# Layer 2 in the written order on five engines, with its other work placed between products

## The chip, the cores and the metric

One core of a Trainium2 chip runs the whole program in one launch. The metric is the device time of one execution in microseconds (us). The core has five instruction queues that matter here: PE (matmuls), ACT (activations, copies), DVE (tensor arithmetic), POOL (tensor arithmetic too, and some DMAs in the attention), SP (here it issues nearly all DMAs). Each queue runs its instructions strictly in its own order; an instruction that waits for another engine's result, or for a buffer, holds up everything behind it on its queue.

## The reference

Attention on q, k, v gives 2304 tokens of 512 values; two feed-forward layers follow, each 512 to 2048 to 512, the second with ELU.

```
def _moe_ref(x, w_in, w_out):
    h = x @ w_in
    g = h * (1.0 / (1.0 + np.exp(-1.702 * h)))
    return (g @ w_out).astype(np.float32)

def _moe2_ref(x, w_in, w_out):
    h = x @ w_in
    g = np.where(h > 0.0, h, np.exp(np.minimum(h, 0.0)) - 1.0)
    return (g @ w_out).astype(np.float32)

def reference(**kwargs):
    attn_out = _attn_ref(**attn_kwargs)
    B, H, S, D = attn_out.shape
    x = np.ascontiguousarray(attn_out.transpose(0, 2, 1, 3)).reshape(B * S, H * D)
    x = _moe_ref(x=x, **moe_kwargs)
    return _moe2_ref(x=x, **moe2_kwargs)
```

## The kernel before

The program runs attention, layer 1 (which overlaps it) and layer 2. Every large matmul operand is split in two parts, hi (ACT copies it to fp32r, a rounded type that TensorE takes) and lo (DVE subtracts hi from the original), and each product is three matmuls: hi by hi, hi by lo, lo by hi. So an operand is ready only after a load, an ACT instruction and a DVE instruction. This pair is called a split below.

Layer 2 is computed block by block, with 7 products in place of 8 for a 2 by 2 block matrix (`PRODUCTS`). The operands of the 7 products are the four blocks A12, A22, A11, A21 and four sums of them, S1 to S4; on the weights' side likewise the blocks and the sums T1 to T3 and N4.

- The tokens are cut in three super blocks, `sb` = 0, 1, 2, each two halves of 256, 384 and 512 tokens (`SUPER`). The hidden dimension is cut in 8 pairs, `p` = 0 to 7.
- First multiplication: one **group** (p, sb) is 7 products, k = 0 to 6, of 6 matmuls each (`group_h2`, line 912). A group's matmuls need `ws` of its p (`split_w7`, L899 on ACT and L900 on DVE; `sum_w7`, L857, forms its four sums) and `xops` of its sb (`load_x`, `sum_x` at L866, `split_x2` at L887/L888). ACT copies the products k = 0 and 4 out of the PSUM bank, DVE adds the other five (L950). Then ELU: Relu and Exp on ACT (L906, L907), the end on DVE (L910), for two of the four quarters ("most") and later for the other two ("rest"); POOL makes the four sums S of the result (L866), and H and S are stored to DRAM (L929, L930) in the memory `gd`. There are 3 H buffers and 2 S buffers: a group's ELU writes into the S buffer, so it waits until the store of two groups earlier has landed.
- Order of groups: (0,0), (1,0), (0,1), (1,1), (0,2), (1,2), then p = 2 to 6 with sb 0, 1, 2, and last (7,1), (7,0), (7,2).
- Second multiplication: for sb = 1, 0, 2 and k = 0 to 6 there are 4 parts (`product_o2`, L1001). A part needs `gs`, the split of a piece `gf` of `gd` (`load_g` L962, `split_g` L968/L969), and `wo(k)`, the split of a 1 MB weight `wof` (`load_wo` L976, `split_wo` L981/L982). The weights are loaded once, while sb = 1 runs; `wof` has one buffer, so the load for k + 1 waits for the DVE half of the split for k.

What sets the order: within layer 2, PE alone runs in the order of the program (`tc.manual_schedule(engines={PE})`, line 1149). On ACT, DVE, POOL and SP a scheduler that has its own idea of durations places the instructions. The last part of a group (rest of ELU, sums, stores) is a function `last`, called once after product 1 of the next group. The operand `xops` of sb 2 is written into the program after group (1,0): four units of 256 columns, one buffer, sums on DVE. At the end of layer 1, in its last block of tokens (steps (5, 0), (5, 1), ...), the scheduler mixes the units of sb 0 (4 of 128 columns, one buffer `xs`, sums on POOL) with layer 1's own ACT and DVE work: g (L704 on ACT, L707 on DVE), which a matmul `h` waits for since h has two PSUM buffers.

## Time and profile before

| quantity | us |
|---|---|
| median of 3 runs | 1065.36 (1062.88 to 1068.53) |
| profiled execution, its own time | 1068.55 |
| its span | 1066.7 |
| PE busy | 962.2 (90% of the span) |
| DVE, ACT, POOL busy | 639.5, 535.3, 243.6 |
| last matmul ends (from the span's start) | 1059.85 |
| layer 2's first matmul starts | 602.77 |

The page cuts the span in 40 slices of 26.7 us; the first rows are PE's busy tenths and the granted TensorE clock in tenths of 2.4 GHz.

```
PE   8988999999999999999999989872898999738999997
PEclk8998999999999999999999995989999869999999
```

PE is busy nearly everywhere, apart from the slices about 600 to 690 and 815 to 880 us, which are the start of layer 2 and the passage from its first to its second multiplication. The clock is low in the same slices. A stage table (busy time of each engine in a stretch) is the view that the reader needs most: the length of a stretch less PE's work there is what a better order could win.

### The profile page before, as it was taken

How to read it: one execution, taken by the hardware profiler on the slowest of the kernel's cores; microseconds unless marked ns; L12 is line 12 of the kernel's file. 1: busy time of each engine (PE TensorE's matmuls, PEld its weight loads, DVE VectorE, ACT ScalarE, POOL GpSimd, SP SyncE). 2: the span in 40 equal slices, each digit the busy share in tenths (PEclk: the TensorE clock that was granted, in tenths of full speed). 3: DMA queues.
4: the chain of work that ended last, by engine and by line, in shares of the span. 5: the costliest groups of instructions: out<-in, count | busy, mean ns of one | idle time of the engine just before them, and what ended most of it. 6: DMA issues, size and time to landing. Idle time of an engine off the chain costs nothing.

```text
span 1066.7 us, 17803 instructions
## 1 busy us (share of the span) xinstructions
PE 962.2 (90%) x6820; PEld 827.0 (78%) x6820; DVE 639.5 (60%) x1029; ACT 535.3 (50%) x1110; POOL 243.6 (23%) x261
## 2 busy tenths in 40 slices
...
PEclk8998999999999999999999995989999869999999
...
GB/s 183 210 163 143 249 40 140 121 146 132 135 152 146 146 112 127 112 301 153 1 60 21 99 131 120 90 174 188 200 183 180 250 220 227 199 187 237 214 182 139
DMA packets 166325, 165.74 MB, mean 155 GB/s; under 512 B 83552, under 2 KB 131296, under 8 KB 165344
## 3 DMA queue, kind: packets, MB, share of 16 engines
...
## 4 chain that ended last, share of the span: by engine, by line
PE 59%; DVE 13%; DMA 10%; ACT 9%; issue 5%; POOL 3%; SPq 0%; POOLq 0%; DVEq 0%; ACTq 0%
PE h L694 15%; PE y L727 14%; PE o2d L1001 4%; PE o2a L1001 3%; PE o2c L1001 3%; PE h2c L937 3%; DMA wof<-wodram 3%; PE h2d L937 3%; PE h2a L937 3%; DMA gf<-gd 2%; DMA w64i<-in_moe_w_in_dram 2%; POOL S L866 2%; PE qk L456 2%; PE busy L778 2%; DMA xs<-ydram 2%
## 5 line engine op out<-in xcount | busy, mean ns | idle before, releaser
L727 PE MATMUL y<-g1h,whl1o 128*128 128x256 f32 (+1 forms) x768 | 216.7, 350 | 2.3 <-ACT g1h L708 1.7
L694 PE MATMUL h<-xh,whl1i 128*128 128x256 f32 (+1 forms) x768 | 172.7, 349 | 6.9 <-DVE g L707 5.3
L727 PEld LDWEIGHTS y<-g1h,whl1o 128*128 128x128 f32 x768 | 135.8, 192 | 21.9 <-issue 4.1
L694 PEld LDWEIGHTS h<-xh,whl1i 128*128 128x128 f32 x768 | 122.4, 191 | 26.1 <-DVE g L707 5.9
L383 POOL DMA_DIRECT2D vd<-in_v_dram x72 | 88.3, 1353 | 223.9 <-PE pv L559 84.5
L727 PE MATMUL y<-g1l,whl1o 128*128 128x256 f32 (+1 forms) x384 | 130.8, 341 | 0.8 <-DVE g1l L709 0.8
L969 DVE TENSOR_TENSOR gs<-gf,gs 128x768 fp32r<-128x768 f32 (+2 forms) x84 | 80.0, 963 | 72.8 <-ACT gs L968 72.5
L968 ACT ACTIVATE gs<-gf 128x768 fp32r<-128x768 f32 (+2 forms) x84 | 70.4, 844 | 86.9 <-DMA gf<-gd 28.3
L937 PE MATMUL h2a<-xops,ws 128*128 128x256 f32 (+2 forms) x288 | 64.5, 362 | 30.2 <-ACT xops L887 22.2
L694 PE MATMUL h<-xl,whl1i 128*128 128x256 f32 (+1 forms) x384 | 89.7, 345 | 0.0
L704 ACT ACTIVATE g<-h 128x512 f32<-128x512 f32 x72 | 43.0, 599 | 86.4 <-PE h L694 77.2
L707 DVE SCALAR_TENSOR_TENSOR g<-g,h 128x512 f32<-128x512 f32 x72 | 49.0, 682 | 62.1 <-ACT g L704 62.0
L937 PEld LDWEIGHTS h2a<-xops,ws 128*128 128x128 f32 x288 | 51.6, 206 | 36.5 <-ACT xops L887 23.1
L727 PEld LDWEIGHTS y<-g1l,whl1o 128*128 128x128 f32 x384 | 73.7, 192 | 7.3 <-DVE g1l L709 1.2
L866 POOL TENSOR_TENSOR S<-H 128x256 f32<-128x256 f32 (+2 forms) x48 | 49.6, 1057 | 130.1 <-DVE H L910 130.1
L937 PE MATMUL h2c<-xops,ws 128*128 128x256 f32 (+2 forms) x288 | 62.0, 353 | 17.4 <-DVE H L950 17.0
L1001 PE MATMUL o2a<-wo,gs 128*128 128x256 f32 x432 | 57.4, 296 | 17.8 <-DMA gf<-gd 13.9
L1001 PEld LDWEIGHTS o2a<-wo,gs 128*128 128x128 f32 x432 | 55.9, 204 | 19.1 <-ACT gs L968 14.9
L708 ACT ACTIVATE g1h<-g 128x512 fp32r<-128x512 f32 x72 | 45.6, 634 | 48.7 <-DVE g L707 47.9
L857 POOL TENSOR_TENSOR w7i<-w7i 128x256 f32<-128x256 f32 x32 | 26.0, 834 | 190.1 <-DMA w7i<-wdi 189.5
L937 PEld LDWEIGHTS h2c<-xops,ws 128*128 128x128 f32 x288 | 49.2, 199 | 24.9 <-DVE H L950 20.8
L694 PEld LDWEIGHTS h<-xl,whl1i 128*128 128x128 f32 x384 | 61.6, 192 | 6.5 <-issue 0.2
...
## 6 DMA issues: line engine op xcount, KB each, us to landing
...
```

The source lines that it names most:

```text
L383: nc.gpsimd.dma_start(out=self.vd[:, :, j, :], in_=src, accum_op=ALU.add)
L694: nc.tensor.matmul(out=ph[:, i, :], lhsT=w_in(1, f, c, wp), rhs=xp[:, c, :], start=(n == 0), stop=(n == 3 * NK - 1),)
L704: nc.scalar.activation(out=g, in_=ph, func=AF.Tanh, scale=0.851)
L707: nc.vector.scalar_tensor_tensor(out=g, in0=g, scalar=1.0, in1=ph, op0=ALU.add, op1=ALU.mult)
L708: nc.scalar.activation(out=gh, in_=g, func=AF.Copy)
L727: nc.tensor.matmul(out=yps[blk][m // nf][:, m % nf, :], lhsT=w_out(1, f, wp)[:, m, :], rhs=gp[:, i, :], start=(st == 0 and n == 0 and m % ...
L857: engine.tensor_tensor(out=at[out_], in0=at[a_], in1=at[b_], op=ALU.subtract)
L866: engine.tensor_tensor(out=s_[:, out_], in0=x, in1=y, op=op)
L937: nc.tensor.matmul(out=ps, lhsT=w[:, wp, slot, c * P:(c + 1) * P], rhs=x[:, xp, c, xi, :], start=(k < 4 and i == 0), stop=(i == 5), skip_g ...
L968: nc.scalar.activation(out=t[:, 0], in_=f, func=AF.Copy)
L969: nc.vector.tensor_tensor(out=t[:, 1], in0=f, in1=t[:, 0].bitcast(F32), op=ALU.subtract)
L1001: nc.tensor.matmul(out=ps[:, ch], lhsT=g[:, gp, j, ch * P:(ch + 1) * P], rhs=woops[k][:, wp, p], start=(k < 4 and p == 0 and i == 0 and ch ...
```

## The change

The change is one of order and of buffers; the sums and products are the same.

1. **Written order.** In layer 2's first multiplication all five engines run in the order of the program (`engines=EVERY`). A group's last part is cut in stages: `last(k)` is called after every product k of the next group: Relu and Exp of the rest at k = 1, its end on DVE and the sums on POOL at k = 2, the store of H at k = 4, that of S at k = 6. Other work is a list of tasks `background`, one after a product of a group: `add(i, k, task)` puts it behind product k of group i.
2. **xops of sb 2.** Eight units of 128 columns with 3 buffers in place of four of 256 with one; unit u is loaded at product 3u, counted from group (0,0), summed on POOL (before: DVE) at 3u + 3, split at 3u + 6.
3. **End of layer 1.** The units of sb 0 get two buffers, are summed on DVE (before: POOL) and are written into the steps (5, 1) to (5, 5) of the last block; `ws` of p = 0 and its sums move there too, from POOL to DVE. Of the units of sb 1, every other one is summed on POOL; three buffers.
4. **Weights of layer 2.** Their four sums go from POOL to DVE, their split stands after product 5 of a later group, the next load at product 6.
5. **Second multiplication.** The pieces `gf`/`gs` of sb 1 live in three buffers of `oeg` on the other side of the memory, which is free before the first multiplication ends; loads run four parts ahead, splits two; the first two weights and pieces are placed in groups (7,0) and (7,2).

```diff
...
     def elu(h, e, rows):
 
         nc.scalar.activation(out=e[:, rows], in_=h[:, rows], func=AF.Relu, scale=-1.0)
         nc.scalar.activation(out=e[:, rows], in_=e[:, rows], func=AF.Exp, scale=-1.0)
 
-        def rest():
-            nc.vector.scalar_tensor_tensor(
-                out=h[:, rows], in0=e[:, rows], scalar=-1.0, in1=h[:, rows], op0=ALU.add, op1=ALU.max
-            )
-
-        return rest
-
-    def group_h2(p, sb, pool):
+    def elu_end(h, e, rows):
+        nc.vector.scalar_tensor_tensor(
+            out=h[:, rows], in0=e[:, rows], scalar=-1.0, in1=h[:, rows], op0=ALU.add, op1=ALU.max
+        )
+
+    MOST, REST = slice(1, 3), slice(0, 4, 3)
+
+    def group_h2(p, sb, pool, before, background):
+
...
-        def last():
-            elu(h, s_, slice(0, 4, 3))()
-            sums(nc.gpsimd, s_, h, A12)
-            nc.sync.dma_start(out=gdram[sb][A12:, :, p, :].rearrange("o p n -> p o n"), in_=h[:, :3])
-            nc.sync.dma_start(out=gdram[sb][:A12, :, p, :].rearrange("o p n -> p o n"), in_=s_)
+        def last(k):
+            if k == 1:
+                elu(h, s_, REST)
+            elif k == 2:
+                elu_end(h, s_, REST)
+                sums(nc.gpsimd, s_, h, A12)
+            elif k == 4:
+                nc.sync.dma_start(out=gdram[sb][A12:, :, p, :].rearrange("o p n -> p o n"), in_=h[:, :3])
+            elif k == 6:
+                nc.sync.dma_start(out=gdram[sb][:A12, :, p, :].rearrange("o p n -> p o n"), in_=s_)
 
...
                 nc.scalar.activation(out=c21, in_=ps, func=AF.Copy)
             elif k == 4:
                 nc.scalar.activation(out=c11, in_=ps, func=AF.Copy)
-                most = elu(h, s_, slice(1, 3))
+                elu(h, s_, MOST)
             else:
...
-            if k == 1 and pending:
-                pending.pop(0)()
-            if k == 5:
-                most()
-        pending.append(last)
+            before(k)
+            if k == 6:
+                elu_end(h, s_, MOST)
+            for task in background.get(k, ()):
+                task()
+        return last
...
-            with tc.tile_pool(name="xs", bufs=1, side="right") as xs:
-                for c in range(2):
-                    for at in range(0, 256, P):
-                        load_x(0, c, at, P, xs)
-                        sum_x(nc.gpsimd, 0, c, at)
-                        split_x2(0, c, at)
-            sum_w7(nc.gpsimd, "i", w7[0])
-            split_w7(0, wa)
-            w7[1] = load_w7(wa, "i", 1)
-            sum_w7(nc.gpsimd, "i", w7[1])
+        elif wa is not None and blk == NBLK - 1:
+
+            if 1 <= f2 <= len(units):
+                load_x(*units[f2 - 1], P, xs0)
+            if 2 <= f2 <= len(units) + 1:
+                sum_x(nc.vector, *units[f2 - 2])
+                split_x2(*units[f2 - 2])
+            if f2 == len(units) + 1:
+                lxs.close()
+            if f2 == 1:
+                sum_w7(nc.vector, "i", w7[0])
+                split_w7(0, wa)
+            if f2 == 2:
+                w7[1] = load_w7(wa, "i", 1)
+            if f2 == 3:
+                sum_w7(nc.vector, "i", w7[1])
...
+            w7[2] = load_w7(wa, "i", 2)
+            with tc.tile_pool(name="xs1", bufs=3, side="right") as xs:
                 for at in range(0, 384, P):
                     for c in range(2):
                         load_x(1, c, at, P, xs)
-                        sum_x(nc.vector, 1, c, at)
+                        sum_x((nc.vector, nc.gpsimd)[c], 1, c, at)
                         split_x2(1, c, at)
-            w7[2] = load_w7(wa, "i", 2)
...
-    xs2 = l2.enter_context(tc.tile_pool(name="xs2", bufs=1, side="left"))
+    xs2 = l2.enter_context(tc.tile_pool(name="xs2", bufs=3, side="left"))
...
+    background = [{} for _ in groups]
+
+    def add(i, k, task):
+        i, k = i + k // 7, k % 7
+        background[i].setdefault(k, []).append(task)
+
+    units = [(2, c, at) for at in range(0, 512, P) for c in range(2)]
+    for u, unit in enumerate(units):
+        at = 3 * u
+        add(0, at, lambda unit=unit: load_x(*unit, P, xs2))
+        add(0, at + 3, lambda unit=unit: sum_x(nc.gpsimd, *unit))
+        add(0, at + 6, lambda unit=unit: split_x2(*unit))
+
+    def load_next(p):
+        w7[p] = load_w7(wa, "i", p)
+
+    add(0, 2, lambda: sum_w7(nc.vector, "i", w7[2]))
+    for p in range(NPAIR - 2):
+
+        i = groups.index((p, 2)) + 1 if p != 1 else groups.index((2, 1))
+        add(i, 5, lambda p=p: split_w7(p + 2, wa if p % 2 == 0 else wb))
+        if p + 3 < NPAIR:
+            add(i, 6, lambda p=p: load_next(p + 3))
+            add(i + 1, 6, lambda p=p: sum_w7(nc.vector, "i", w7[p + 3]))
+
+    with tc.manual_schedule(engines=EVERY):
+        before = lambda k: None
+            before = group_h2(p, sb, hpool2, before, background[i])
...
+                oeg = ltail.enter_context(tc.tile_pool(name="oeg", bufs=3, side="right"))
+                j = i + 1
+                add(j, 0, lambda: load_wo(0, wa))
                 for part in range(2):
-                    load_g(1, 0, part, oeg)
-                    split_g(1, 0, part, oeg)
-        for last in pending:
-            last()
+                    add(j, 2, lambda part=part: load_g(1, 0, part, oeg))
+                add(j, 6, lambda: split_wo(0, oe, "wo0"))
+                add(j, 6, lambda: load_wo(1, wa))
+                add(j + 1, 0, lambda: split_g(1, 0, 0, oeg))
+                add(j + 1, 2, lambda: split_g(1, 0, 1, oeg))
+                add(j + 1, 3, lambda: split_wo(1, wa, "ws"))
+                add(j + 1, 3, lambda: load_wo(2, wa))
+                add(j + 1, 4, lambda: load_g(1, 0, 2, oeg))
+                add(j + 1, 6, lambda: load_g(1, 0, 3, oeg))
+        split_g(1, 0, 2, oeg)
+        for k in range(7):
+            before(k)
...
+        order = [(sb, k) for sb in (1, 0, 2) for k in range(7)]
+        sequence = [(sb, k, part) for sb, k in order for part in range(4)]
+        loads, splits = sequence[4:], sequence[3:]
...
+        for i, (sb, k) in enumerate(order):
             for part, _ in enumerate(product_o2(sb, k, opool, op)):
 
                 at = sequence.index((sb, k, part))
+                while loads and sequence.index(loads[0]) <= at + 4:
+                    load_g(*loads[0], oeg if loads.pop(0)[0] == 1 else gp)
                 while splits and sequence.index(splits[0]) <= at + 2:
-                    split_g(*splits.pop(0), gp)
-                    if loads:
-                        load_g(*loads.pop(0), gp)
+                    split_g(*splits[0], oeg if splits.pop(0)[0] == 1 else gp)
...
```

The line numbers in the second kernel are higher: L704 to L737 and L866 to L888 are as before, the copies and additions L943, L945 and L950 become L952, L954 and L959, Relu and Exp L906/L907 become L909/L910, `gs` L968 becomes L978, `wo` L981 becomes L991, `wof` L976 becomes L986, `gf` L962 becomes L972.

On ACT at the end of layer 1, from the first unit of sb 0 (`xops_6150`, named by its `xs` unit) to the first g of block 5, before:

```order
L887 ACTIVATE xops_6150<-xs_0_0_6154 128x7x128
L736 ACTIVATE ye_4_6095<-y_4_5592 128x512
L736 ACTIVATE ye_4_6101<-y_4_5593 128x512
L736 ACTIVATE ye_4_6107<-y_4_5594 128x512
L887 ACTIVATE xops_6150<-xs_0_128_6163 128x7x128
L704 ACTIVATE g_5_0_6135<-h_5_0_6110 128x512
L704 ACTIVATE g_5_1_6233<-h_5_1_6208 128x512
```

and now:

```order
L887 ACTIVATE xops_6150<-xs_0_0_6189 128x7x128
L887 ACTIVATE xops_6150<-xs_1_0_6257 128x7x128
L736 ACTIVATE ye_4_6101<-y_4_5593 128x512
L736 ACTIVATE ye_4_6107<-y_4_5594 128x512
L704 ACTIVATE g_5_0_6135<-h_5_0_6110 128x512
L708 ACTIVATE g1h_0_6137<-g_5_0_6135 128x512
```

In both, two units stand ahead of the first g. Before, the second was xs_0_128, which shares one buffer with the first; now it is xs_1_0, which has a buffer of its own.

On POOL at the start of layer 2, where `xs` are the units and `S_0`, `S_1` the sums of a group of sb 0 or 1, before:

```order
L866 TENSOR_TENSOR xs_0_128_6163<-xs_0_128_6163 128x128 x4
L866 TENSOR_TENSOR xs_1_0_6172<-xs_1_0_6172 128x128 x4
L866 TENSOR_TENSOR xs_1_128_6181<-xs_1_128_6181 128x128 x4
L857 TENSOR_TENSOR w7i_6647<-w7i_6647 128x256 x4
L866 TENSOR_TENSOR S_0_6725<-H_0_6724 128x256 x2
L866 TENSOR_TENSOR S_0_6725<-S_0_6725,H_0_6724 128x256
L866 TENSOR_TENSOR S_0_6725<-H_0_6724,S_0_6725 128x256
L866 TENSOR_TENSOR S_0_6783<-H_0_6782 128x256 x2
L866 TENSOR_TENSOR S_0_6783<-S_0_6783,H_0_6782 128x256
L866 TENSOR_TENSOR S_0_6783<-H_0_6782,S_0_6783 128x256
```

and now:

```order
L866 TENSOR_TENSOR xs_0_0_6738<-xs_0_0_6738 128x128 x4
L866 TENSOR_TENSOR xs_1_0_6770<-xs_1_0_6770 128x128 x4
L866 TENSOR_TENSOR S_0_6726<-H_0_6725 128x256
L866 TENSOR_TENSOR S_0_6726<-S_0_6726,H_0_6725 128x256
L866 TENSOR_TENSOR S_0_6726<-H_0_6725 128x256
L866 TENSOR_TENSOR S_0_6726<-H_0_6725,S_0_6726 128x256
L866 TENSOR_TENSOR xs_0_128_6803<-xs_0_128_6803 128x128 x4
L866 TENSOR_TENSOR xs_1_128_6846<-xs_1_128_6846 128x128 x4
L866 TENSOR_TENSOR xs_0_256_6879<-xs_0_256_6879 128x128 x4
L866 TENSOR_TENSOR S_0_6807<-H_0_6806 128x256
L866 TENSOR_TENSOR S_0_6807<-S_0_6807,H_0_6806 128x256
L866 TENSOR_TENSOR S_0_6807<-H_0_6806 128x256
L866 TENSOR_TENSOR S_0_6807<-H_0_6806,S_0_6807 128x256
L866 TENSOR_TENSOR xs_1_256_6919<-xs_1_256_6919 128x128 x4
```

The four sums of group (0,0), then those of (1,0), now stand among the units of sb 2, of which eight are to be done; before, POOL did the units of sb 0 and nothing of sb 2.

On ACT in the second multiplication, sb 1, where `gs_k_part` is the split of a piece and `wo` that of a weight, before:

```order
L968 ACTIVATE gs_1_0_8520<-gf_1_0_8471 128x768
L981 ACTIVATE wo_8796<-wof_8700 128x2048
L968 ACTIVATE gs_1_1_8543<-gf_1_1_8477 128x768
L1011 ACTIVATE ot_1_8567<-o2a_8473 128x3x256
L968 ACTIVATE gs_1_2_8570<-gf_1_2_8500 128x768
L968 ACTIVATE gs_1_3_8593<-gf_1_3_8523 128x768
L981 ACTIVATE wo_8894<-wof_8799 128x2048
L968 ACTIVATE gs_2_0_8621<-gf_2_0_8546 128x768
L968 ACTIVATE gs_2_1_8644<-gf_2_1_8573 128x768
L968 ACTIVATE gs_2_2_8669<-gf_2_2_8596 128x768
L981 ACTIVATE wo_8992<-wof_8897 128x2048
```

and now, from the weight of k = 2 on:

```order
L991 ACTIVATE wo_8633<-wof_8454 128x2048
L978 ACTIVATE gs_2_0_8658<-gf_2_0_8605 128x768
L978 ACTIVATE gs_2_1_8681<-gf_2_1_8628 128x768
L978 ACTIVATE gs_2_2_8706<-gf_2_2_8656 128x768
L978 ACTIVATE gs_2_3_8729<-gf_2_3_8679 128x768
L991 ACTIVATE wo_8732<-wof_8636 128x2048
L978 ACTIVATE gs_3_0_8757<-gf_3_0_8704 128x768
L978 ACTIVATE gs_3_1_8780<-gf_3_1_8727 128x768
L978 ACTIVATE gs_3_2_8805<-gf_3_2_8755 128x768
L978 ACTIVATE gs_3_3_8828<-gf_3_3_8778 128x768
L991 ACTIVATE wo_8831<-wof_8735 128x2048
```

Before, the three weights of these rows (k = 4 to 6) follow each other after three or four pieces each, and all are ahead of the pieces of k = 2 and 3. Now one weight stands behind the four pieces of each k, so that the weight of k + 1 is split while product k runs.

On SP at the same place (`gf` are the loads of pieces, `wof` those of weights), before:

```order
L976 DMA wof_8700<-wodram 128x2048
L962 DMA gf_1_1_8477<-gd_101 128x768
L962 DMA gf_1_2_8500<-gd_101 128x768
L962 DMA gf_1_3_8523<-gd_101 128x768
L976 DMA wof_8799<-wodram 128x2048
L962 DMA gf_2_0_8546<-gd_101 128x768
L962 DMA gf_2_1_8573<-gd_101 128x768
L962 DMA gf_2_2_8596<-gd_101 128x768
L976 DMA wof_8897<-wodram 128x2048
L962 DMA gf_2_3_8624<-gd_101 128x768
```

and now:

```order
L972 DMA gf_2_0_8605<-gd_101 128x768
L972 DMA gf_2_1_8628<-gd_101 128x768
L986 DMA wof_8636<-wodram 128x2048
L972 DMA gf_2_2_8656<-gd_101 128x768
L972 DMA gf_2_3_8679<-gd_101 128x768
L972 DMA gf_3_0_8704<-gd_101 128x768
L972 DMA gf_3_1_8727<-gd_101 128x768
L986 DMA wof_8735<-wodram 128x2048
L972 DMA gf_3_2_8755<-gd_101 128x768
L972 DMA gf_3_3_8778<-gd_101 128x768
```

The last two pieces of each k now stand behind the weight of k + 1.

## Rows read from the trace of the kernel before

**Rows 1.** Stages: us, busy (count) of PE, PEld, DVE, ACT, POOL; PEclk, DMA share, GB/s.
```profile
602.80:715.40 112.60, 77.61 (x378) 68.34 (x379) 68.63 (x103) 48.89 (x62) 40.64 (x43) 0.82 0.38 131
...
715.40:815.80 100.40, 91.59 (x506) 82.43 (x505) 62.89 (x88) 56.19 (x77) 59.01 (x60) 0.98 0.53 189
...
815.80:848.00 32.20, 24.39 (x127) 21.21 (x125) 21.94 (x27) 17.76 (x24) 16.62 (x13) 0.93 0.65 226
...
848.00:887.80 39.80, 22.10 (x145) 21.23 (x145) 16.28 (x12) 15.60 (x14) 7.04 (x4) 0.71 0.63 228
...
887.80:936.40 48.60, 45.10 (x362) 44.49 (x363) 26.72 (x28) 19.71 (x23) 0.00 (x0) 0.96 0.63 198
...
936.40:980.40 44.00, 41.90 (x339) 40.42 (x337) 22.11 (x33) 18.51 (x29) 0.00 (x0) 1.00 0.60 204
```

**Rows 2.** Chain that ended last, in order of time: start, us, what.
```profile
722.33 0.71 PE h2d L937 x6
...
723.05 1.04 PE h2a L937 x6
...
731.72 1.40 PE h2b L937 x6
...
851.41 5.77 POOL S L866 x3
...
859.02 7.25 DMA wof<-wodram
...
879.70 4.75 DMA wof<-wodram
...
919.13 8.64 PE o2c L1001 x72
```

**Rows 3.** Timeline at layer 1's end: start, us, engine, line, op [idle before <-releaser].
```profile
552.20 0.92 SPq L876 DMA_DIRECT2D xs<-ydram  x2
...
555.38 1.82 POOL L866 TENSOR_TENSOR xs<-xs 128x128 f32<-128x128 f32 x4 [5.32 <-DMA xs<-ydram]
...
557.24 0.95 ACT L887 ACTIVATE xops<-xs 128x896 fp32r<-128x896 f32 x1 [2.92 <-POOL xs L866]
...
559.96 0.99 PE L694 MATMUL h<-xh,whl1i 128*128 128x256 f32 x4 [4.04 <-DVE g L707]
...
561.61 1.91 PE L694 MATMUL h<-xh,whl1i 128*128 128x256 f32 x8
```

**Rows 4.** Timeline of PE at the start of layer 2.
```profile
608.19 1.65 PE L937 MATMUL h2a<-xops,ws 128*128 128x256 f32 x6 [2.28 <-ACT H L943]
...
660.83 1.22 PE L937 MATMUL h2a<-xops,ws 128*128 128x512 f32 x2 [8.07 <-ACT xops L887]
```

**Rows 5.** Groups by line and form: busy us, mean ns | idle before.
```profile
L866 POOL TENSOR_TENSOR S<-H 128x256 f32<-128x256 f32 x16 | 11.5, 739 | 21.2 <-DVE H L910 21.2
...
L866 POOL TENSOR_TENSOR S<-H,S 128x256 f32<-128x256 f32 x8 | 7.9, 993 | 0.6
...
L866 POOL TENSOR_TENSOR xs<-xs 128x128 f32<-128x128 f32 x16 | 7.0, 459 | 54.0 <-DMA xs<-ydram 53.7
...
L887 ACT ACTIVATE xops<-xs 128x896 fp32r<-128x896 f32 x10 | 9.4, 949 | 17.0 <-POOL xs L866 10.5 <-DVE xs L866 6.4
...
L888 DVE TENSOR_TENSOR xops<-xs,xops 128x896 fp32r<-128x896 f32 x10 | 11.3, 1146 | 19.0 <-ACT xops L887 19.0
...
L982 DVE TENSOR_TENSOR wo<-wof,wo 128x2048 fp32r<-128x2048 f32 x7 | 16.9, 2408 | 27.1 <-ACT wo L981 27.1
```

**Rows 6.** Timeline of ACT in the second multiplication, sb 1.
```profile
866.28 1.91 ACT L981 ACTIVATE wo<-wof 128x2048 fp32r<-128x2048 f32 x1 [14.32 <-DMA wof<-wodram]
...
868.10 2.29 ACT L968 ACTIVATE gs<-gf 128x768 fp32r<-128x768 f32 x3
...
884.48 1.91 ACT L981 ACTIVATE wo<-wof 128x2048 fp32r<-128x2048 f32 x1 [4.24 <-DMA wof<-wodram]
...
886.88 2.73 ACT L968 ACTIVATE gs<-gf 128x768 fp32r<-128x768 f32 x3 [0.49 <-DMA gf<-gd]
```

42 lines of the change are left out of this document (11 added, 31 removed).

## The prediction

> **What bounds the kernel now.** I read the granted clock and the share of PE first: PE is busy nearly all the time, so only stretches where it stands still, or runs at half clock, can give anything. The stage table then says which [rows 1]. PE's pure work there is a count: at full clock a product of 6 matmuls takes 0.72, 1.04 or 1.40 us (256, 384, 512 columns) and one of 72 in the second multiplication of sb 1 takes 8.64 [rows 2], so a group takes 5.0, 7.3 or 9.8 and a whole p 22.1. From layer 2's first matmul to the start of (3,0) there are 9 groups, 66.4 us of products in 112.6: 46 us are lost. p = 3 to 6 take 100.4, or 25.1 each for 22.1. p = 7 takes 32.2 for 22.1. The second multiplication of sb 1 takes 39.8 + 48.6 = 88.4 for 7 products of 8.64, or 60.5. sb 0 takes 44.0 for about 40. sb 2 has no idle time and the change leaves it so.
>
> Then the timelines and the chain, for what each loss waits on. At layer 1's end PE stands 4.04 us, then runs 8 matmuls in 1.91 us, half rate [rows 3]. At layer 2's start PE stops for ACT's copy, and the 6 matmuls behind the stop span 1.65 us, twice the usual [rows 4]; the granted clock is 0.82 over this stage [rows 1]. Later it waits for xops of sb 2, which come through one buffer, the last time 8.07 us. At the passage to the second multiplication the chain goes through POOL's sums and weight loads [rows 2].
>
> **The change part by part.** Before's profiled execution is the base: 1068.55 us, 3.2 above the median, so differences are taken from it and applied to the median.
>
> *Layer 1's end.* SP's unit load of 552.20, late since the one buffer was full, gives POOL's sums at 555.38, ACT's split at 557.24, and behind that on ACT the first g, which h waits for until 559.96 [rows 3]. The order now has two units of separate buffers ahead of g, which can both be loaded long before, so g waits for no unit and PE need not stop or lose its clock. At most this saves 4.04 and the half rate: 4 matmuls in 0.99 and 8 in 1.91, at 0.12 each (8.64 by 72) 0.5 and 1.0 too long, 1.5 together. Later units still stand ahead of other g's and wait on loads, for which I take off 0.5: **-5.0**, bounds -5.5 and 0 (the wait comes back at the next g).
>
> *Start of layer 2.* POOL's sums become the path to xops of sb 2. Eight units are 32 x 0.459 = 14.7 us; in the written order the sums of (0,0) and (1,0) (about 4 x 0.74 = 3.0 each) and (0,1) (half as much again, 4.4) stand among them [rows 5]: 25.1 us. The first unit's load waits for memory that the last split of sb 1 frees, which I place some 11 us into layer 2, with 3 to 4 us to load it: POOL starts at about 617.5, an estimate, and would end at 642.6. But each of these S sums waits for a group's ELU end, and so for PE's own stops, while units behind it lie ready. I put 8 us on these waits, an estimate: three groups each have 2 to 4 us of stops, like the 2.28 at 608 [rows 4]. With 0.95 + 1.15 for the last split [rows 5] it makes 652.7, and with half a product's delay on the way some 654.5, where before (0,2) got its last wait over at 660.83 [rows 4] and a lo part 2 us later: -8.4. Of it 2.3 go again up to (3,0). The split of p = 2 has one `ws` buffer and can start only when (1,2) is done: seven eighths of a `wo` split, 1.7 on ACT and 2.1 on DVE [rows 5, 6], 4 us with PE idle. And the Relu of (2,1) waits for the store of (1,2), put at 3. With half rate behind both that is some 11 us of the 13.1 lost from (0,2) to (3,0); before lost 11 there (52.5 less 41.7 of products). Sum **-6.1**, bounds +2 (all of it lost in the waits) and -16 (no waits on POOL).
>
> *p = 3 to 6.* POOL is busy 59.0 of 100.4 us [rows 1]; the S buffers still are two, and the store of S still gates the Relu two groups later. Taking the weight sums off POOL brings the sums forward, but the stores now are issued after product 4 and 6. I find no net: **0**, bounds -10 (2.5 of the 3.0 us lost per p) and +4.
>
> *p = 7.* The weights and pieces are placed from (7,0) on. What was lost, 10.1, becomes about 6.9: stops on H and S stores in (7,2), and half clock: **-3.2**. *sb 1, k = 0 and 1.* PE now waits at part 2 of k = 0 (its piece is queued on SP behind `wof` of k = 2, which waits for DVE's split of k = 1), some 8 us, and at k = 1 (its piece behind the store of S(7,2), which waits for POOL's sums, 5.77 for three ops before [rows 2]), some 10; before lost 22.5 (39.8 less 17.3). **-1.2**. For both together bounds -9 and +6.
>
> *sb 1, k = 2 to 6.* Here the written order costs. Before, weights were split well ahead of their products (the order has those of k = 4 to 6 in front of most pieces of k = 2), so that k = 3 to 6 ran at 8.64 each [rows 2]. Now a loop closes: DVE ends `wo(k+1)`; only then SP issues `wof(k+2)`, 4.75 to landing when alone [rows 2]; two pieces are queued behind it; ACT must split both before it may split the weight (the order shows it), 1.91 [rows 6]; DVE ends it after 2.41 in the mean [rows 5], and SP can go on. The pieces: three pieces queued behind a weight were split straight after it at 868.10, so the first was there 1.8 after the weight, while at 886.88 ACT waited for it until 2.4 after [rows 6]. The second a little later: 2.4 after the weight is my value, between 1.0 and 3.3. The loop: 4.75 + 2.4 + 0.90 + 1.91 + 2.35 = 12.3, with the hand-overs 12.4. Four loops and one free product: 4 x 12.4 + 8.64 = 58.2, against 48.6 before: **+9.6**, bounds -0.4 (9.9 per loop, pieces there when the weight is split) and +14. The Trainium skill (DMA: Bandwidth & Descriptors, Anatomy of one DMA) gives about 2.0 us fixed per DMA, measured for another kind of queue, plus bytes at 436 GB/s: 4.4 for the weight, near the 4.75 of the trace. If only the moving part counts for pieces queued behind, as that split suggests, the two take 1.8, not 2.4, and the sum would be 2.4 us lower.
>
> *sb 0.* Three buffers as before, and the same loop of load, ACT and DVE per 3 parts; the loads are issued ahead of the splits now: -0.5, bounds -4 (all that is lost there) and +4.
>
> Sum: -5.0 - 6.1 + 0 - 3.2 - 1.2 + 9.6 - 0.5 = **-6.4**. The profiled execution would be at 1062.1, the median at 1059.0.
>
> **Rivals.**
> *The loop does not bind* (faster). If the pieces land within ACT's 1.9 us of the weight's split, as at 868.10, the loop is 9.9 and the term -0.4: -16.4 in all, 1049. Against it: the order puts the pieces ahead of the weight, and at 886.88 one was late.
> *The entry gives nothing* (no change). If POOL's waits cost 16 us and not 8, (0,2) starts where it did: +8.4, so +2.0, 1067. For it: any stop of PE there comes back through ELU and POOL's order. The by-form rows also show the same sum at 0.739 and 0.993 [rows 5], so POOL's ops stretch in some places. The Trainium skill (SBUF — State Buffer, SBUF: two separate sides) says that a DVE op with two SBUF inputs and a POOL op that reads SBUF shut each other out, which fits that pair of rows; DVE's eight lo splits, 9.2 us, now lie beside POOL's 25 and could add up to that, giving 1068.
> *The in-order SP queue makes loads late* (slower). Six places (part 2 of k = 0, the start of k = 1, four loops) hold PE until a load lands behind another transfer. A weight took 4.75 alone but 7.25 at 859.02, beside the stores of (7,2) [rows 2]: 2.5 us more. At 2.5 in six places: +15, so +8.6, 1074. From 2.0 each (+12) it decides for slower. Against it: sb 1's stores are over when the loops run, so only the first two places are sure to share.
>
> **How the numbers follow.** Chances: forecast 0.45 (1053 to 1066 by its own bounds), loop hidden 0.20, entry gives nothing 0.20, loads late 0.15. A measurement here can tell about 0.5% (5.3 us) from no change: faster is below 1060.0, slower above 1070.7. The forecast lies on that edge and gives 0.28 faster, 0.15 same, 0.02 slower; the loop hidden 0.20 faster; the entry 0.02, 0.13, 0.05; loads late 0.01 same, 0.14 slower. So 0.50, 0.29, 0.21. Range 1045 to 1072: below to the loop hidden with a little of p = 3 to 6's gain, above to the slower case less a part.
>
> **What would show it.** Right: PE without the 4 us stop near 556; (0,2) starting 6 to 10 us earlier, counted from layer 2's first matmul, with POOL idle before S sums; p = 3 to 6 at 25 each; in sb 1 a stop of PE in each k from 2 to 5 at parts 2 and 3 or at the next k, k to k 12 us, ACT's `wo` right behind the split of part 3; sb 0 at 44. Wrong: k to k at 8.64 or 10 (loop), (0,2) at 60 us from layer 2's start or more (entry), p = 3 to 6 under 23.5 each (then two S buffers and POOL were not the limit).

## The result, and the profile after

| | median us | runs | ratio to before |
|---|---|---|---|
| before | 1066.81 (1062.49 to 1070.91) | 20 | |
| after | 1071.48 (1067.77 to 1080.23) | 20 | 1.006 [1.004, 1.0079] |

The change makes the kernel slower by 0.6% (0.4 to 0.8); 0.6% faster (-6.4 us) was forecast. The profiled span grew by 7.2 us, from 1066.7 to 1073.9, more than the medians (4.7 us), since the profiled execution of after was one of its longer ones. Its stages say where. A stage ends where PE's first matmul of the next one starts (the waits ahead of a stage count to the one before):

| stage, us | before | after | difference | forecast |
|---|---|---|---|---|
| last block of layer 1 to layer 2 | 52.8 | 50.3 | -2.5 | -5.0 |
| start of layer 2, to (3,0) | 112.7 | 101.6 | -11.1 | -6.1 |
| p = 3 to 6 | 100.3 | 109.4 | +9.1 | 0 |
| p = 7 | 32.3 | 35.0 | +2.7 | -3.2 |
| sb 1, k = 0 and 1 | 39.7 | 34.1 | -5.6 | -1.2 |
| sb 1, k = 2 to 6 | 48.5 | 58.0 | +9.5 | +9.6 |
| sb 0 | 42.9 | 45.5 | +2.6 | -0.5 |
| sb 2, to its k = 6 | 69.0 | 71.7 | +2.7 | 0 |

The sum is +7.4; the other 0.2 lies ahead of layer 1's last block. The stage table of after, which answers to [rows 1], has per stretch the time, busy (count) of PE, PEld, DVE, ACT and POOL, granted clock, DMA share, GB/s:

```profile
599.90:701.50 101.60, 79.35 (x378) 68.50 (x379) 60.90 (x86) 48.01 (x65) 54.44 (x70) 0.88 0.40 134
701.50:810.90 109.40, 97.22 (x505) 87.03 (x504) 70.98 (x104) 57.48 (x77) 57.40 (x51) 0.94 0.48 168
810.90:846.00 35.10, 26.73 (x128) 22.41 (x126) 21.44 (x27) 18.07 (x23) 13.57 (x13) 0.85 0.60 200
846.00:880.10 34.10, 21.88 (x145) 20.77 (x146) 11.36 (x11) 10.93 (x12) 5.66 (x4) 0.80 0.59 202
880.10:938.10 58.00, 49.74 (x362) 47.82 (x361) 30.86 (x29) 24.05 (x25) 0.00 (x0) 0.91 0.64 221
938.10:983.60 45.50, 41.63 (x339) 40.54 (x337) 21.24 (x33) 18.45 (x29) 0.00 (x0) 1.00 0.60 203
```

In p = 3 to 6 PE is busy 97.2 us, before 91.6, with the same matmuls at a mean clock of 0.94 for 0.98: some six of the nine lost microseconds are a slower clock, the rest waits.

**The stop that costs there.** The timeline of after around a stop in (4,1), engines together (start, us, engine, line, operation, idle time before it and what ended it):

```profile
736.44 1.69 ACT L904 ACTIVATE ws<-w7i 128x1792 fp32r<-128x1792 f32 x1
...
738.16 2.45 DVE L905 TENSOR_TENSOR ws<-w7i,ws 128x1792 fp32r<-128x1792 f32 x1 [2.76 <-ACT ws L904]
740.53 0.41 DVE L959 TENSOR_TENSOR H<-H,h2d 128x256 f32<-128x256 f32 x1
740.86 1.44 DVE L913 SCALAR_TENSOR_TENSOR H<-S,H 128x512 f32<-128x512 f32 x1
...
742.87 0.55 DVE L959 TENSOR_TENSOR H<-H,h2c 128x384 f32<-128x384 f32 x1
...
743.48 2.03 PE L946 MATMUL h2c<-xops,ws 128*128 128x384 f32 x6 [2.14 <-DVE H L959]
```

DVE's half of the weight split stands first in its queue and waits 2.76 us for ACT's half, which ACT could not start earlier: in front of it stand the Relu and Exp of the group (735.24 and 735.91), which wait for a DVE addition. Behind the waiting split stands a ready addition (740.53; its product is done before 736.2), then the end of an ELU, then the additions of (4,1). PE's product 5 of (4,1) adds into the PSUM bank of product 2, whose addition comes only at 742.87: PE stops 2.14 us, and likewise in each p. The wait is not all of the delay: beside POOL's sums the split takes 2.45 us (before 2.02) and the ELU end 1.44 (0.68 at 743.34 in the same timeline), 1.2 us together.

Before lost as much once in each p, 2.11 to 2.17 in (p,0), behind a DVE that was busy and not waiting (timelines of before, (4,0); the split has no idle time before it):

```profile
742.35 2.02 DVE L900 TENSOR_TENSOR ws<-w7i,ws 128x1792 fp32r<-128x1792 f32 x1
...
745.76 0.41 DVE L950 TENSOR_TENSOR H<-H,h2c 128x256 f32<-128x256 f32 x1
...
746.23 0.98 PE L937 MATMUL h2c<-xops,ws 128*128 128x256 f32 x6 [2.11 <-DVE H L950]
```

What differs is the clock behind the stop. The 3 us behind the stop in p = 3, 4, 5, 6, before and then after (columns as above):

```profile
721.40:724.40 3.00, 3.00 (x21) 3.00 (x22) 1.90 (x4) 2.12 (x4) 3.00 (x3) 1.00 0.97 364
746.30:749.30 3.00, 3.00 (x21) 3.00 (x22) 1.87 (x4) 2.15 (x4) 3.00 (x3) 1.00 0.97 367
771.10:774.10 3.00, 3.00 (x15) 3.00 (x16) 1.51 (x4) 1.47 (x3) 3.00 (x3) 0.63 0.98 371
797.20:800.20 3.00, 3.00 (x21) 3.00 (x22) 1.90 (x4) 2.12 (x4) 3.00 (x3) 1.00 0.96 380
```

```profile
716.70:719.70 3.00, 3.00 (x10) 3.00 (x11) 1.49 (x3) 0.00 (x0) 2.38 (x4) 0.50 0.99 266
743.50:746.50 3.00, 3.00 (x10) 3.00 (x11) 1.54 (x3) 0.00 (x0) 2.32 (x4) 0.55 0.99 266
770.40:773.40 3.00, 3.00 (x11) 3.00 (x12) 1.57 (x3) 0.00 (x0) 2.29 (x4) 0.62 0.99 266
797.40:800.40 3.00, 3.00 (x12) 2.93 (x13) 1.48 (x3) 0.48 (x1) 2.38 (x4) 0.67 1.01 363
```

The clock fell to 1.2 GHz behind one of four stops before, behind four of four after; the chain of waits has the products there at up to 2.29 where [rows 2] has 1.04. From start to start, the three products behind each of the four stops take 6.7 us too long in after and 1.8 in before. With a second stop of about 0.5 in each p (at 735.13, waiting on an addition behind an ELU end) and one of 1.54 in (3,0) alone, it makes 6.7 - 1.8 + 2.0 + 1.5 = 8.4 of the 9.1. A p takes 26.9, the first 28.6.

Some of the 9.1 is luck of the two profiled executions. Three kernels of experiment 3, whose edits leave this stage as it is in before, had two falls of the clock in four stops and took 101.7 to 102.7; two with after's order here (the loop edits of experiments 1 and 4) had three falls and took 108.5. So 6 to 7 us are the change's.

**The loop of sb 1.** Chain of waits of after, k = 2 to 4 (start, us, what), which answers to the single 4.75 and 8.64 of [rows 2]:

```profile
879.72 6.19 DMA gf<-gd
886.01 0.84 ACT gs L978
886.86 1.81 ACT wo L991
888.69 2.30 DVE wo L992
891.90 7.17 DMA gf<-gd
899.17 0.84 ACT gs L978
900.02 1.81 ACT wo L991
901.85 2.30 DVE wo L992
```

This is the loop as forecast: weight and pieces landing, ACT on the piece, ACT on the weight, DVE on the weight, next load. The products of k = 2 to 6 start 12.2, 13.5, 10.3 and 13.6 us apart, 12.4 in the mean; 12.4 was the forecast. The loop itself is steadier: the weight splits on DVE that start at 888.69 and 901.85 are 13.2 apart, the ones before and behind them 12.2 and 12.1.

**The entries.** At layer 1's end PE no longer stops before h, and the last y matmul ends some 5.5 us earlier. The next waits take half of it back (timeline of ACT and PE, after):

```profile
598.45 0.95 ACT L887 ACTIVATE xops<-xs 128x896 fp32r<-128x896 f32 x1 [1.44 <-DVE xs L866]
599.30 0.58 ACT L736 ACTIVATE ye<-y 128x512 f32<-128x512 f32 x1
...
599.93 1.25 PE L946 MATMUL h2a<-xops,ws 128*128 128x256 f32 x6 [3.95 <-ACT ye L736]
```

The last copy `ye` stands on ACT behind splits of sb 1's units. Layer 2's start, POOL's timeline and the first product of sb 2 in PE's, which answers to 660.83 of [rows 4]:

```profile
612.28 4.99 POOL L866 TENSOR_TENSOR xs<-xs 128x128 f32<-128x128 f32 x8 [6.18 <-DMA xs<-ydram]
618.55 1.45 POOL L866 TENSOR_TENSOR S<-H 128x256 f32<-128x256 f32 x1 [1.28 <-issue]
...
622.18 6.76 POOL L866 TENSOR_TENSOR xs<-xs 128x128 f32<-128x128 f32 x12
631.16 0.73 POOL L866 TENSOR_TENSOR S<-H 128x256 f32<-128x256 f32 x1 [2.22 <-DVE H L913]
...
634.03 5.83 POOL L866 TENSOR_TENSOR xs<-xs 128x128 f32<-128x128 f32 x8
640.78 1.01 POOL L866 TENSOR_TENSOR S<-H 128x384 f32<-128x384 f32 x1 [0.92 <-DVE H L913]
...
646.18 1.80 POOL L866 TENSOR_TENSOR xs<-xs 128x128 f32<-128x128 f32 x4
```

```profile
649.01 2.77 PE L946 MATMUL h2a<-xops,ws 128*128 128x512 f32 x5 [6.24 <-ACT xops L887]
```

POOL starts 12.4 us into layer 2 (14.7 was put) and waits 1.28 + 2.22 + 0.92 for ELU ends, not 8 (the profile names no releaser for the first, but DVE's ELU end of (0,0) is done at 618.41). Its 32 operations on units take 19.4 us, not 14.7, and all its work to the last unit 31.3, not 25.1; it is done 48.1 us into layer 2, where 47.8 was forecast. The wait for `xops` ends 49.1 us after layer 2's first matmul, before 58.1.

### The profile page after: what moved, and what is told of

The parts are those of the page before. It is cut to its first block, busy times and chain, and to the rows that moved or that the text cites. A ratio compares the mean times of both kernels' runs of the same rounds, so it can differ in the third digit from the quotient of the medians.

```text
span 1073.9 us, 17811 instructions
## 1 busy us (share of the span) xinstructions
PE 976.1 (91%) x6820; PEld 836.5 (78%) x6820; DVE 645.0 (60%) x1053; ACT 536.5 (50%) x1114; POOL 239.8 (22%) x257
## 5 line engine op out<-in xcount | busy, mean ns | idle before, releaser
L383 POOL DMA_DIRECT2D vd<-in_v_dram x72 | 88.2, 1332 | 223.5 <-PE pv L559 101.7
L978 ACT ACTIVATE gs<-gf 128x768 fp32r<-128x768 f32 (+2 forms) x84 | 70.8, 843 | 126.9 <-DMA gf<-gd 80.6
L704 ACT ACTIVATE g<-h 128x512 f32<-128x512 f32 x72 | 43.1, 599 | 90.2 <-PE h L694 80.7
L866 POOL TENSOR_TENSOR xs<-xs 128x128 f32<-128x128 f32 x44 | 25.1, 595 | 262.3 <-DVE xs L866 248.6
L946 PE MATMUL h2c<-xops,ws 128*128 128x256 f32 (+2 forms) x288 | 65.2, 366 | 19.9 <-DVE H L959 19.9
L866 POOL TENSOR_TENSOR S<-H 128x256 f32<-128x256 f32 (+2 forms) x48 | 51.1, 1064 | 120.6 <-DVE H L913 119.3
L946 PE MATMUL h2d<-xops,ws 128*128 128x256 f32 (+2 forms) x288 | 65.6, 368 | 6.3 <-DVE H L959 6.2
L909 ACT ACTIVATE S<-H 128x512 f32<-128x512 f32 (+2 forms) x48 | 40.4, 842 | 51.3 <-DMA gd<-S 24.5
```

The source lines that it names most:

```text
L383: nc.gpsimd.dma_start(out=self.vd[:, :, j, :], in_=src, accum_op=ALU.add)
L704: nc.scalar.activation(out=g, in_=ph, func=AF.Tanh, scale=0.851)
L866: engine.tensor_tensor(out=s_[:, out_], in0=x, in1=y, op=op)
L909: nc.scalar.activation(out=e[:, rows], in_=h[:, rows], func=AF.Relu, scale=-1.0)
L946: nc.tensor.matmul(out=ps, lhsT=w[:, wp, slot, c * P:(c + 1) * P], rhs=x[:, xp, c, xi, :], start=(k < 4 and i == 0), stop=(i == 5), skip_g ...
L978: nc.scalar.activation(out=t[:, 0], in_=f, func=AF.Copy)
```

## The experiments

Stage times of an experiment are those of its one profiled execution.

**1. Where the 9 us of p = 3 to 6 come from.** Three edits of after, one of the loop, and one that puts only PE in the written order.

Weight split later, behind product 3 of (p + 1, 1):

```diff
-        i = groups.index((p, 2)) + 1 if p != 1 else groups.index((2, 1))
-        add(i, 5, lambda p=p: split_w7(p + 2, wa if p % 2 == 0 else wb))
+        i = groups.index((p + 1, 1)) if p else groups.index((1, 2))
+        add(i, 3, lambda p=p: split_w7(p + 2, wa if p % 2 == 0 else wb))
...
-            add(i, 6, lambda p=p: load_next(p + 3))
-            add(i + 1, 6, lambda p=p: sum_w7(nc.vector, "i", w7[p + 3]))
+            add(i, 4, lambda p=p: load_next(p + 3))
+            add(i + 1, 2 if p else 6, lambda p=p: sum_w7(nc.vector, "i", w7[p + 3]))
```

> The changed kernel with one thing moved: the split of ws(p+2) (ACT 1.7, DVE 2.0 to 2.5 us) goes from product 5 of the small group (p+1,0) to product 3 of (p+1,1), with its load and sums behind it. Theory A (the DVE half of this split stands in front of DVE's additions of the small group, so that product 5 of (p,1) waits 2.15 us and then runs at half rate): the stop and the half rate go, p = 3 to 6 fall from 27.3 us each to 22.5 to 23.5, the kernel gains 15 to 20 us on the changed one and is 8 to 14 us faster than the kernel before. Rival B (the stop comes from DVE and POOL shutting each other out, since L913 took 1.44 beside POOL's sums and 0.70 alone, or from the wait for the store of S): the stop stays within 1 us wherever the split is, 26 us or more for each p, the time within 4 us of the changed kernel.

Measured: ratio 0.9988 [0.9967, 1.0009], p = 3 to 6 in 102.3, or 25.6 each: between theory and rival, and the gain of 5.6 us on after is short of the 15 to 20. So the placing of the split cost 7 us. At its new place the split, whole and 2.31 us long, waits for nothing, and PE has no stop in that group. But a stop came at (p,2) in p = 3 to 5, where the weight's four sums now lie beside POOL's (timelines of this kernel):

```profile
709.93 2.31 DVE L905 TENSOR_TENSOR ws<-w7i,ws 128x1792 fp32r<-128x1792 f32 x1
...
718.19 3.85 DVE L857 TENSOR_TENSOR w7i<-w7i 128x256 f32<-128x256 f32 x4
...
718.35 1.13 POOL L866 TENSOR_TENSOR S<-H 128x384 f32<-128x384 f32 x1 [4.12 <-DVE H L913]
...
722.69 2.42 PE L946 MATMUL h2d<-xops,ws 128*128 128x512 f32 x6 [2.33 <-DVE H L959]
```

Weight split of sb 1 ahead of the two pieces:

```diff
+                if part == 0 and k + 1 in wo_at and i < 7:
+                    split_wo(k + 1, *wo_at[k + 1])
+                    if k + 2 < 7:
+                        load_wo(k + 2, wa)
                 while splits and sequence.index(splits[0]) <= at + 2:
                     split_g(*splits[0], oeg if splits.pop(0)[0] == 1 else gp)
-                if part == 1 and k + 1 in wo_at and i < 7:
...
```

> The changed kernel with one thing moved: in sb 1 of the second multiplication the split of wo(k+1) is written ahead of the splits of parts 2 and 3 of product k, not behind them. Loop theory (weight load 4.75, two pieces queued behind it 2.4, split of a piece 0.9, weight split 1.9 and 2.3, then the next weight load): the pieces leave the loop, k to k falls from 12.2 to about 9.1, and the kernel is 11 to 14 us faster than the changed one, 4 to 8 faster than the kernel before. Rival (the DMA queues are simply full there, 221 GB/s, and PE would wait for the pieces instead): k to k stays at 11 or more, at most 5 us gained.

Measured: ratio 1.0016 [0.9989, 1.0043]; k = 2 to 6 went from 58.0 to 54.3, k to k from 12.4 to 11.4 in the mean (10.9, 10.8, 10.9, 13.1), and the kernel gained 2.3 us: the rival's numbers, not the 9.1 of the loop theory. The pieces leave the loop, but a new one closes: the chain shows DVE's split of a piece, then a load of a piece of 4.84 to 4.92, then ACT on it, once per k. The rival's reason, full queues, is not shown: the DMA share of after is 0.64 in this stage, and 0.97 to 1.01 behind the stops of p = 3 to 6.

More PE work where the stop is (product 4 of the groups (3,1) to (6,1) issued twice, so that the result counts it double):

```diff
+            fill = k == 4 and sb == 1 and 3 <= p <= 6
-            for wp, xp in ((0, 0), (0, 1), (1, 0)):
+            for wp, xp in ((0, 0), (0, 1), (1, 0)) * (2 if fill else 1):
...
-                        start=(k < 4 and i == 0), stop=(i == 5), skip_group_check=True,
+                        start=(k < 4 and i == 0), stop=(i == (11 if fill else 5)), skip_group_check=True,
```

> The changed kernel with six matmuls more: product 4 of the groups (3,1) to (6,1) is issued twice into its bank (so that c11 there counts it double), 1.04 us of PE work in front of the stop of 2.15 us. Clock theory (half of what p = 3 to 6 lost is no stop but the lower granted clock after it, which comes from PE standing still): the stop shrinks to 1.1, the half rate goes, p = 3 to 6 fall from 27.3 to about 25, the kernel with more work is 8 to 9 us faster than the changed one. Rival (the clock falls whatever PE does there, or the added products push everything back): no gain, or 4 us slower.

Measured: 0.9992 [0.9973, 1.0012]. With 24 matmuls more, 4.2 us of work, p = 3 to 6 fell from 109.4 to 104.5. The stop is 1.14 to 1.48 us and the clock never falls (stage table of this kernel):

```profile
696.40:800.90 104.50, 95.71 (x530) 84.65 (x529) 69.44 (x104) 57.56 (x77) 56.07 (x51) 1.00 0.50 175
```

Less the added work these four p take 100.3, as before's did. Since the added work fills a part of the stop, this shows that stop and clock are enough for the +9.1, not that each microsecond is theirs; nor does it part the two. The kernel gained 5.6 us on after, not the 8 to 9 expected.

Written order for PE alone, all else of after kept:

```diff
-    with tc.manual_schedule(engines=EVERY):
+    with tc.manual_schedule(engines={mybir.EngineType.PE}):
```

> The changed kernel with the written order on PE alone in layer 2, as the kernel before has it; the scheduler places ACT, DVE, POOL and SP again. All buffers, units and placements in the program stay. If the written order is what costs (p = 3 to 6 at 27.3, the loop of sb 1 at 12.2), these stages go back to about 25 and 9 us, and the kernel is 15 to 25 us faster than the changed one if the start of layer 2 keeps its gain of 11 us. Rival (the stages' order follows from the buffers and the positions in the program, so that the scheduler ends near the same): within 5 us of the changed kernel.

Measured: 0.9762 [0.9723, 0.98], 1041.64 us. The written order on the other four engines costs 30 us; all the rest of the change is worth 25. By stage against after: start of layer 2 92.7 (from (0,2) to (3,0) 48.5 for 59.1), p = 3 to 6 104.5, p = 7 30.7, k = 0 and 1 30.3, k = 2 to 6 52.7, sb 0 41.2. The gain is above the 15 to 25 expected, but p = 3 to 6 did not go back to 25 each: 4.2 of the 9.1 stay, with stops of 2.16 to 2.44 in (p,0) and the clock down behind three of the four.

**2. Which engine's order.** The same line with PE and one more engine in the set: SP, POOL, DVE, ACT.

```diff
-    with tc.manual_schedule(engines=EVERY):
+    with tc.manual_schedule(engines={mybir.EngineType.PE, mybir.EngineType.SP}):
```

> The changed kernel with the written order on PE and SP alone; the scheduler places ACT, DVE and POOL. With PE alone it ran at 1041.6, with all five at 1071.5. If SP's queue (weight and piece loads behind stores and behind each other) carries the 30 us, this is at 1062 to 1072; if the compute engines' order does, at 1040 to 1048. I expect the latter with some of SP's loop left: 1046, k to k in sb 1 at 10 to 12.

> The changed kernel with the written order on PE and POOL alone. If POOL's order carries the start of layer 2 (units of sb 2 behind the sums S of a group that wait for its ELU end), the stretch from (0,0) to (3,0) is about 100 us as with all five, against 92.7 with PE alone, and the rest as with PE alone: 1047 to 1050. If POOL only follows DVE's order, 1040 to 1044.

> The changed kernel with the written order on PE and DVE alone. If DVE's order (ws split and weight sums ahead of the additions that PE waits for) carries the loss in p = 3 to 6, these take 27 us each as with all five, against 26.1 with PE alone, and the kernel 1046 to 1052. If what DVE waits for on ACT decides, 1040 to 1045.

> The changed kernel with the written order on PE and ACT alone. If ACT's order (the weight's split behind the splits of parts 2 and 3, Relu and Exp of the rest ahead of copies) closes the loop of sb 1 by itself, k to k is 11 to 12.5 for k = 2 to 6 and the kernel at 1050 to 1060. If SP and ACT are needed together, 1040 to 1047.

Measured: SP 1062.48, 0.997 [0.9945, 0.9995]; POOL 1045.92, 0.9806 [0.9774, 0.9838]; DVE 1046.93, 0.9819 [0.9788, 0.985]; ACT 1057.36, 0.9916 [0.9888, 0.9945]. Against 1041.64 each alone costs 21, 4, 5 and 16 us. They sum to 46, not 30, so they overlap. SP and ACT carry most: the queue that issues loads, and the one whose half of each split comes first. The SP run is where its queue theory put it, not at the 1046 expected; in the ACT run k to k is 10.4, not 11 to 12.5, so that loop is not what ACT's order costs. Against PE alone, POOL's order costs 8.5 us at the start of layer 2 (101.2), ACT's 10.3 there (103.0) and 8.2 in p = 3 to 6 (112.7), DVE's 5.2 in p = 3 to 6 (109.7), and SP's most in sb 0 (48.1) and in k = 0 and 1 (35.3). In the DVE and the ACT run the split of `ws` waits 0.29 us at most, and p = 3 to 6 is as slow as in after by other stops (in the DVE run 1.91 to 2.26 in (p,2), for ACT's copy). So the wait for ACT is what costs in the order of after; it is not the only way to lose these 9 us. In the POOL run the stop of 2.15 us is there in each p too, and the clock behind it was 1.00, 0.55, 0.75, 1.00: the same stop with and without the fall.

**3. The parts alone, on before.** Part 3 (with its release of constants' memory, as in the next two), part 2, part 5's buffers, each put into before, whose scheduler stays; and after with PE alone written, as above, with the weight split in three pieces:

```diff
-    xs2 = l2.enter_context(tc.tile_pool(name="xs2", bufs=1, side="left"))
+    xs2 = l2.enter_context(tc.tile_pool(name="xs2", bufs=3, side="left"))
...
-                oeg = ltail.enter_context(tc.tile_pool(name="oeg", bufs=2, side="right"))
+                oeg = ltail.enter_context(tc.tile_pool(name="oeg", bufs=3, side="right"))
...
-        nc.scalar.activation(out=hi, in_=w, func=AF.Copy)
-        nc.vector.tensor_tensor(out=lo, in0=w, in1=hi.bitcast(F32), op=ALU.subtract)
+        for r in (slice(0, 2), slice(2, 4), slice(4, 7)):
+            nc.scalar.activation(out=hi[:, r], in_=w[:, r], func=AF.Copy)
+            nc.vector.tensor_tensor(out=lo[:, r], in0=w[:, r], in1=hi[:, r].bitcast(F32), op=ALU.subtract)
```

> The kernel before with part 3 alone (end of layer 1: two buffers and DVE for the units of sb 0, weights moved, units of sb 1 with three buffers) and the earlier release of the attention's constants. By the trace of the changed kernel the stop of 4.04 us and its half rate go (5.5 us), but ACT's last output copy then stands behind a unit of sb 1 and layer 2 starts 3.9 us late: from the first matmul of block 5 to layer 2 50.4 us in place of 52.8. Theory: 2 to 3 us faster than before, 1063 to 1064.5. Rival (the 4 us come back in the stages behind, where the units of sb 1 now are summed on POOL): no change or slower, 1066 to 1068.

> The kernel before with part 2 alone (xops of sb 2 in eight units with three buffers, summed on POOL, two units behind each of the first four groups). (0,2) waited 23 us for units through one buffer before; with three the loads lie beside each other. Theory: (0,2) starts 10 to 15 us earlier, counted from layer 2's first matmul, the kernel is at 1051 to 1057. Rival (POOL's sums become the path, 25 us of work): 2 to 6 us earlier, 1060 to 1064.

> The kernel before with the buffers of part 5 alone (three buffers of oeg for all pieces of sb 1, loads four parts ahead, splits two), the scheduler placing them, and the earlier release of constants. Before, the first parts of sb 1 had two such buffers and then waited for the memory of the first multiplication (13.86 us at the third part). Theory: that wait goes, sb 1 falls from 88.2 to about 78 us, kernel 1055 to 1058. Rival (the wait is for POOL's sums of (7,2), whose store stands ahead on SP, not for memory): less than 3 us, 1063 to 1067.

> The changed kernel with the written order on PE alone (1041.6) and the split of ws cut in three pieces on ACT and DVE, so that no instruction of 2.0 us stands in front of the additions that product 5 of a small group waits for. Theory (DVE's one long instruction makes the stop of 2.16 us, which costs half rate too in about every second p): the stop falls under 1.2 us, p = 3 to 6 from 26.1 to 23.5 to 25 us, the kernel 1034 to 1039. Rival (the ELU end of the group of sb 2, 1.23 us, and the locks with POOL keep the additions late): the stop stays at 2 us, 1040 to 1043.

Measured: part 3 0.9951 [0.9925, 0.9977], its block in 52.0 for 52.8 and the start of layer 2 in 108.8 for 112.7; part 2 0.9893 [0.9846, 0.994], 1057.51, just above its range, the start of layer 2 in 101.8, as in after; part 5's buffers 0.9853 [0.9819, 0.9887], 1053.84, below its range, though sb 1 takes 81.3 and not 78: k = 0 and 1 in 27.5 for 39.7, k = 2 to 6 in 53.8 for 48.5; three pieces 0.9644 [0.9611, 0.9677], 1031.56, p = 3 to 6 in 97.4, better than its theory. There the stops are 0.39 and 1.53 and the clock holds (stage table of that kernel, nearly all of it in p = 3 to 6):

```profile
690.00:790.00 100.00, 94.12 (x518) 83.52 (x517) 82.13 (x111) 58.80 (x87) 49.78 (x47) 1.00 0.54 190
```

So parts 2, 3 and 5 each gain under the scheduler, and the written order on engines other than PE loses. How much of each gain is the part's own stays open. All three kernels also end the memory of the attention's constants earlier, as after does (the list of the change leaves it out), and no run has that alone; in the third, which edits nothing else at the start of layer 2, that start fell to 105.5 from 112.7.

**4. Is it the long instruction or the wait?** The theory after the third set was that the unbroken 2.45 us of DVE's split is what stands in the way. Pieces in the written order:

```diff
-        add(i, 5, lambda p=p: split_w7(p + 2, wa if p % 2 == 0 else wb))
+        add(i, 4, lambda p=p: (open_w7(p + 2, wa if p % 2 == 0 else wb), piece_w7(p + 2, slice(0, 2))))
+        add(i, 5, lambda p=p: piece_w7(p + 2, slice(2, 4)))
+        add(i, 6, lambda p=p: piece_w7(p + 2, slice(4, 7)))
```

> The changed kernel, written order on all five engines, with the split of ws in three pieces behind products 4, 5 and 6 of the same group, so that DVE's additions stand between pieces of 0.6 to 0.9 us. If the one long DVE instruction is what turned p = 3 to 6 from 25.1 to 27.3 us each (stops of 0.5 and 2.15 us and the half rate behind them), the stretch falls from 109.4 to 97 to 101 us and the kernel from 1071.5 to 1060 to 1064. If ACT's place for the split, or the store of S, decides, it stays above 106 and the kernel above 1068.

Measured: 1.0057 [1.0035, 1.0079], p = 3 to 6 in 108.3. The theory fell (timelines of DVE and PE in this kernel):

```profile
761.70 0.93 DVE L903 TENSOR_TENSOR ws<-w7i,ws 128x512 fp32r<-128x512 f32 x1 [2.02 <-ACT ws L902]
762.55 0.41 DVE L967 TENSOR_TENSOR H<-H,h2c 128x256 f32<-128x256 f32 x1
...
768.07 1.92 PE L954 MATMUL h2c<-xops,ws 128*128 128x384 f32 x6 [2.15 <-DVE H L967]
```

The first piece, at 0.93 long, waits for ACT as the whole did, and in three of the four p the stop is 2.15 as in after. Cut and still waiting, the split costs the stop; whole and not waiting (experiment 1), it does not. So in this order it is the wait, not the length. Under the scheduler, where nothing waited, the same pieces took p = 3 to 6 from 104.5 to 97.4: there the length did count.

The order on SP in the second multiplication, splits and weight ahead of the loads (in the written order, then with the pieces under the scheduler, then with the pieces and the weight first in the written order):

```diff
-                while loads and sequence.index(loads[0]) <= at + 4:
-                    load_g(*loads[0], oeg if loads.pop(0)[0] == 1 else gp)
                 while splits and sequence.index(splits[0]) <= at + 2:
                     split_g(*splits[0], oeg if splits.pop(0)[0] == 1 else gp)
+                while loads and sequence.index(loads[0]) <= at + 5:
+                    load_g(*loads[0], oeg if loads.pop(0)[0] == 1 else gp)
```

> The changed kernel with the piece loads of the second multiplication written behind the splits and five parts ahead, as the kernel before had it (the load into a buffer right behind the split that frees it), in place of ahead of them and four parts ahead. Theory: SP then has one more piece ahead of each weight load, so the loop of sb 1 loses one piece (0.8 to 1.2 us of 12.2), and sb 0 goes back from 45.5 to about 43 us: 5 to 7 us faster than the changed kernel, 1064 to 1067. Rival (sb 0 is slow because of the buffers' side of the memory or of the DMA queues): within 3 us.

> The kernel with PE alone in the written order and ws in three pieces (1031.6) with the piece loads written behind the splits, five parts ahead. The scheduler places them, so little should move: 1029 to 1033; if the order in the program sets the order of loads, 3 to 5 us faster, 1027 to 1029.

> The written order on all five engines with the three corrections: ws in three pieces, the weight's split ahead of the splits of parts 2 and 3, piece loads behind the splits. If the losses found are separate, they add: 8 to 12 for p = 3 to 6, 4 for the loop (e2 gave 3.7 in its stage), 3 for sb 0: 1052 to 1058, faster than the kernel before. If the written order costs in general (start of layer 2 and passages too), it cannot reach 1041.6, which PE alone gave.

Measured: 0.9968 [0.9945, 0.9992], 1063.50, just below its range, k = 2 to 6 in 53.5 and sb 0 in 43.7, so SP's order there cost some 6 us; 0.9677 [0.9649, 0.9706], 1030.60, the lowest median of all, which these intervals don't part from the 1031.56; 0.9987 [0.9967, 1.0007], 1065.40 and not the 1052 to 1058 expected, with k = 2 to 6 in 54.1 and p = 3 to 6 in 108.4: the two cures of the loop don't add, and the pieces give 1 us.

**5. The wait taken away.** In the written order still: ACT's half goes where ACT idles, behind product 2 of (p + 1, 2), and DVE's, in three pieces, only behind products 3, 4 and 5, when ACT's is done. The second kernel has the order on SP above as well.

```diff
-        i = groups.index((p, 2)) + 1 if p != 1 else groups.index((2, 1))
-        add(i, 5, lambda p=p: split_w7(p + 2, wa if p % 2 == 0 else wb))
+        i = groups.index((p + 1, 2))
+        add(i, 2, lambda p=p: hi_w7(p + 2, wa if p % 2 == 0 else wb))
+        for k, r in ((3, slice(0, 2)), (4, slice(2, 4)), (5, slice(4, 7))):
+            add(i, k, lambda p=p, r=r: lo_w7(p + 2, r))
...
-            add(i + 1, 6, lambda p=p: sum_w7(nc.vector, "i", w7[p + 3]))
+            add(i + 2, 6, lambda p=p: sum_w7(nc.vector, "i", w7[p + 3]))
```

> The changed kernel, written order on all five engines, with the split of ws(p+2) moved to where both engines stand idle in the trace: ACT's half behind product 2 of (p+1,2), in a gap of 3.4 us before the copy of product 4, DVE's half in three pieces behind products 3, 4 and 5; the next load and its sums follow. h1_pieces showed that the length of DVE's instruction is not it: DVE stood 2.02 us before the first piece, waiting for ACT behind Relu and Exp, with a ready addition behind it (2.76 us with one piece). Theory (the wait in the in-order queue decides, not the work): the stops of 0.51 and 2.15 us and the half rate go, p = 3 to 6 fall from 109.4 to 92 to 98 us, the kernel to 1055 to 1061. Rival (the store of S, 4.3 us of wait on ACT, takes over): 102 to 106, 1064 to 1068.

> i1_where_idle with the piece loads of h2_swap (behind the splits, five parts ahead), which gave 6 us by themselves in their two stages. If the two are separate: 6 us below i1, 1049 to 1055, the best with the written order on all five engines. If not, within 3 us of i1.

Measured: 0.9962 [0.993, 0.9993], 1062.14, and 0.9839 [0.9783, 0.9895], 1050.95 as expected. In the first p = 3 to 6 takes 101.1 for 109.4, short of the 92 to 98 of the theory and just below the rival's 102 to 106. Stage table of the first, most of it in p = 3 to 6, then PE's largest stop in its timeline around (5,0):

```profile
700.00:800.00 100.00, 93.07 (x497) 81.38 (x496) 76.17 (x111) 56.91 (x76) 54.42 (x48) 1.00 0.53 184
```

```profile
745.14 0.50 PE L954 MATMUL h2b<-xops,ws 128*128 128x256 f32 x2 [1.29 <-DVE ws L906]
```

With the wait gone from DVE's queue the 2.15 us stop is gone, the clock holds, and 8.3 of the 9.1 us come back, all five engines still in the written order. A shorter stop comes in its place: PE waits 1.29 us for the last piece of `ws`, which is now ready only when (5,0) needs it. This edit cuts the split, too, and moves it into a group of longer products, as experiment 1 moved it; no run takes the wait away at the old place, so what the longer products give is not parted from it.

## Why the prediction was wrong

The forecast was 1059.0, faster; it came out slower. That the time lies inside the range is luck: against their terms p = 3 to 6, p = 7, layer 1's end, sb 0 and sb 2 came out 23.3 us dearer, and the start of layer 2 and k = 0 and 1 9.4 cheaper. Its sum of -6.4 had the right sign in four of its six terms other than 0; the rest decided.

- **p = 3 to 6, "I find no net: 0", is the step that failed.** It measured +9.1, beyond its bound of +4. The step counted POOL's work and the S buffers and left out the move of `ws` in DVE's queue: behind a wait for ACT. The rule was in the prediction for sb 1, where a loop of such waits was followed, and was not put to this place. Experiments 1, 4 and 5 show it: moving the split to where it does not wait gives 7 us, cutting it where it waits gives 1, cutting and moving it so that no piece waits 8.3. The step also took no account of the clock, which in before fell behind only one of four such stops.
- **p = 7, -3.2, came out +2.7.** The 6.9 us of loss that it put there were read from no row. Chain of waits and PE's timeline of after:

```profile
822.36 8.70 DMA wof<-wodram
831.08 1.92 ACT wo L991
```

```profile
833.52 2.93 PE L946 MATMUL h2a<-xops,ws 128*128 128x512 f32 x6 [3.82 <-ACT H L952]
```

  The weight took 8.70 to land, and ACT, in order, had its split in front of the copy that PE needed; then a product of 512 columns spans 2.93 where 1.56 is usual (at 828.14), half rate behind a stop again. The "loads late" rival had this mechanism, at 2.5 us more than the 4.75 of a weight alone where it was 3.95, but not this place.
- **Layer 1's end, -5.0, came out -2.5.** The 4.04 us stop went and the half rate with it, as said; the 0.5 taken off for later waits was 2.5 too small: PE stands 3.95 us ahead of layer 2, where before stood 0.75.
- **sb 0 and sb 2, -0.5 and 0, came out +2.6 and +2.7.** In sb 0 it is the order on SP: with splits ahead of loads it is 43.7, 1.8 less. Most of the +2.6 is the last wait, for the first piece of sb 2, 2.34 where before had 0.60. In sb 2 the granted clock is 0.86 over the 12 us from 985 on (before 1.00), and the first product is longer; the next ones are too (chain of after):

```profile
984.85 13.04 PE o2a L1011 x94
997.89 11.52 PE o2b L1011 x96
```

  Before's first took 11.24 and its next three 11.20. None of the +2.7 in sb 2 is shown to be the change's. The next products take 11.5 in every other kernel here, those with before's order among them. The first does not follow the stop: from start to start it is 14.1 in after and 12.3 in before, but also 14.1 with part 5's buffers alone, behind a wait of 0.74, and 12.6 with the pieces of experiment 4, behind one of 2.48.
- **Start of layer 2, -6.1, came out -11.1**: right in its mechanism, and under-sized behind it. The last wait of (0,2) ended 9.0 earlier, where 8.4 was put, by errors that offset each other: POOL began 2.3 earlier and waited 3.6 less, but worked 6.2 longer. The term that failed is the 2.3 that were to be lost again up to (3,0): there 2.1 were gained.
- **sb 1, k = 0 and 1, -1.2, came out -5.6**, inside the bounds. The two waits that the prediction names, 8 and 10 for 22.5, make -4.5 and not the -1.2 that it wrote: the working was better than its sum. Part 5's buffers are enough for it, since in before they shorten it by more (27.5 for 39.7).
- **The loop of sb 1, +9.6, came out +9.5**, k to k 12.4 as worked out: the one term that followed a waiting instruction to its successors.

Of the rivals, "the loop does not bind" fell with the 12.4; "the entry gives nothing" fell with the -11.1, though POOL's units were stretched, 19.4 for 14.7. "Loads late" has 1074, near what was measured, by luck: of its six places the first two together came out 4.4 us below the forecast and the four loops at it. None had the weight split of p = 3 to 6.

**What stays open.** Why the clock falls behind a 2.15 us stop in one case and not in another; what the earlier end of the constants' memory gives alone; which of ACT's instructions cost the 10.3 and 8.2 us that its order alone costs in two stages; whether the split could stay in (p,0) if only its wait were gone.
